# A Fourier-mixing and cosine-gated MLP kernel: another order of its opening

## The chip, the cores and the metric

The kernel runs on one core of one Trainium2 chip. The metric is the time of one execution on the device, in microseconds. A core has five engines that run side by side and wait for each other through semaphores: TensorE (PE in the profile; PEld is its loading of weights), VectorE (DVE), ScalarE (ACT), GpSimd (POOL) and SyncE (SP), which here issues nearly all DMAs. Each engine works through its own instructions in the order in which the program gives them.

## The reference

x has the shape (8, 3008, 256). Each of the 8 batches goes through a Fourier transform along its 3008 rows and another along its 256 columns, and the real part is kept. Each of the 24064 rows of 256 then goes through a small network:

```python
X = np.fft.fft(np.fft.fft(x, axis=1), axis=2).real     # (24064, 256)
h = X @ w_in                                           # w_in (256, 2048)
g = h * np.cos(h)
out = g @ w_out                                        # w_out (2048, 256)
```

All inputs and the output are float32.

## The kernel before, in words

**Transform along the rows.** 3008 is split as 47 x 64. For each batch x is loaded in four pieces (`load_x(b, p)`, L140), each with 8 of 32 forward columns and their mirrored partners; the mirrored half is read backwards in rows of 1 KB. A piece gives two chunks. `fold` (L226) adds and subtracts the two halves of the 256 columns: for batch 0 on VectorE, with GpSimd copying two columns, for later batches on GpSimd alone. `first_half` (L249) multiplies a chunk with the table `L` of length 47 into `pz` (PSUM, buffers of tag M), and `keep_z` (L285) copies it to `zs` on ScalarE. `store_z` (L322) writes zs to DRAM, and `load_z` (L334) reads it back with other axes on the partitions: z travels through DRAM. `second_half(b, g)` (L346) multiplies z with the table `BJ`, for a group g of four values of j, into `pb`; copies on ScalarE give `pq`, the transformed columns of group g. One row of pq is also spread over all partitions as `nb`, through DRAM (L376, L377) or, for the first group, by a matmul (`spread_nb`, L380).

**Transform along the columns.** It is not done on x: it is folded into w_in. `weights(e, n)` (L417) multiplies quarter n of w_in (512 of 2048 columns) with the table `CS`, giving a cosine part `WC` (e=0) and a sine part `WS` (e=1), 2 x 2 matmuls of 128 x 512 a quarter; `keep_weights` (L429) copies them to SBUF on ScalarE. Row 0 of WS holds another coefficient that is needed as columns over the partitions: `weight_row(n)` (L436) turns it with four matmuls into four columns of the tile `wn`, `keep_wn` (L449) copies these on ScalarE, and GpSimd sets the row to zero (L454).

**The main loop.** There are 8 batches x 6 groups x 8 blocks of w_in's columns = 384 steps, each in two halves; the loop (L847) runs over halves k, and t = k // 2 is the step. A half passes through a pipeline: `seed` (ScalarE, L504) writes nb times a column of wn into its PSUM tile H; `mm1` (L525) adds WC and WS products of pq; `act_e` and `dve_h` make the two mirrored values h; `act_round`, `dve_frac`, `act_sin` and `dve_g` make g = h cos h; `sums` (GpSimd, L581) makes sums of g, and `mm2` (L599) multiplies them with w_out, in combinations (`VX`, `combine_w2`, L487) that need 7 products instead of 8. mm2 of a step starts LAG = 5 halves after its first half. Half k reads column k of wn in the first group, so halves 4, 8 and 12 are the first to read what quarters 1, 2 and 3 give. The first two halves have no seed: a memset and a product with `wrow` (`seed_first`, L514) stand in for it. Halves 1 to 4 seed the next half ahead of their round (L886), later ones behind it (L894).

**The order of the work** is written out by hand, and every engine keeps it. The opening stands in lines 758 to 845: fill-in matmuls on ones (`keep_busy`), chunks, first halves, weight quarters and DMA issues; quarter 3 is folded inside the loop at k = 0, 1 and 2 (L861). `opening` (L812) is a table of calls at the end of step t. `transform(b)` (L391) is the same for the next batch: `load_x(1, p)` at t = 2p, `store_z`, `load_z` and `second_half` later. So SyncE's queue holds, one behind another: the loads of x and weights of batch 0, the stores and loads of z, quarter 3 and w_out (`load_w2`), the rest of z (j from 4 on), the rest of w_out and BJ, and then x of batch 1.

Of the kernel before, what the change touches and what calls it, by code (L numbers as in the profile page):

```python
# [11 lines left out]
FP = mybir.dt.float32  # L12
# [6 lines left out]
ND = 256  # L19
NDFF = 2048  # L20
N2 = 47
NJ = 24
# [3 lines left out]
XP = 2 * IP  # L26
NG = 6
LAG = 5
AHEAD = LAG + 1
# [79 lines left out]
def kernel(  # L109
# [7 lines left out]
    nc = tc.nc  # L117
# [22 lines left out]
    def load_x(b, p):  # L140
        if (b, p) not in xs:
            take_x(b, p)
        xt = xs[b, p]
        xv = xt.rearrange("r (i d) -> r i d", d=ND)
        i0 = XP * p
        for r0, r1 in ((0, 32), (32, 47)):
            nc.sync.dma_start(out=xv[r0:r1], in_=x_r[b, r0:r1, i0 : i0 + XP, :])
            q0, q1 = N2 + r0, N2 + r1
            if p == 0:
                nc.sync.dma_start(out=xv[q0:q1, 0:1], in_=x_r[b, r0:r1, 32:33, :])  # L150
                nc.sync.dma_start(
                    out=xv[q0:q1, 1:XP], in_=x_r[b, r0:r1, 63 : 64 - XP : -1, :]
                )
            else:
                nc.sync.dma_start(
                    out=xv[q0:q1], in_=x_r[b, r0:r1, 64 - i0 : 64 - i0 - XP : -1, :]
                )


    CS = [cpool.tile([128, 256], FP, tag=f"CS{i}", name=f"CS{i}") for i in range(2)]  # L160
    wr = [
        [spool.tile([128, 7 * 256], FP, tag=tag, bufs=1, name="wr") for tag in ("mr", "cb")],
    ]
    L = cpool.tile([128, 256], FP, tag="L", name="L")
    BJ = cpool.tile([128, NJ * 128], FP, tag="BJ", name="BJ")
    w2 = cpool.tile([128, 16 * ND], FP, tag="w2", name="w2")
# [5 lines left out]
    def load_w(q):  # L172
        for i in range(2):
            nc.sync.dma_start(
                out=wr[q // 2][i][:, 512 * (q % 2) : 512 * (q % 2) + 512],
                in_=moe_w_in[i * 128 : (i + 1) * 128, 512 * q : 512 * q + 512],
            )

    def load_bj(c0, c1):
        nc.sync.dma_start(out=BJ[:, c0:c1], in_=B_dr.ap()[:, c0:c1])  # L180
# [11 lines left out]
    load_x(0, 0)  # L192
    load_cs()
    load_w(0)
    load_x(0, 1)
    WC = cpool.tile([128, NDFF], FP, tag="WC", name="WC")
    WS = cpool.tile([128, NDFF], FP, tag="WS", name="WS")
    wn = cpool.tile([128, 16], FP, tag="wn", name="wn")
# [120 lines left out]
    zds = {}  # L319
    z2s = {}  # L320

    def store_z(b, c, j0=0, j1=NJ):  # L322
        half, q = divmod(c, NCH // 2)
        if q == 0 and j0 == 0:
            zds[b, half] = dpool.tile([32, 2 * NJ * 128], FP, tag="zd", bufs=4, name="zd")
        zd, zs = zds[b, half], zss[b, c]
        for e in range(2):
            p0 = 16 * e + IP * q
            nc.sync.dma_start(
                out=zd[p0 : p0 + IP, 256 * j0 : 256 * j1].rearrange("i (y d) -> y i d", d=128),  # L330
                in_=zs[64 * e + 2 * j0 : 64 * e + 2 * j1, :].rearrange("y (i d) -> y i d", d=128),
            )

    def load_z(b, half, j0=0, j1=NJ):  # L334
        if b not in z2s:
            z2s[b] = spool.tile([128, NJ * 128], FP, tag="z2", bufs=1, name="z2")
        for r in range(2):
            p0 = 64 * half + 32 * r
            nc.sync.dma_start(
                out=z2s[b][p0 : p0 + 32, 128 * j0 : 128 * j1].rearrange("i (j d) -> i j d", d=128),  # L340
                in_=zds[b, half].rearrange("i (j r d) -> r i j d", r=2, d=128)[r, :, j0:j1],
            )
# [71 lines left out]
    def fold_weights(e, n, tag="M"):  # L414
        keep_weights(e, n, weights(e, n, tag))

    def weights(e, n, tag="M"):  # L417
        pw = psum("pw", tag)
        for i in range(2):
            nc.tensor.matmul(  # L420
                pw,
                lhsT=CS[i][:, 128 * e : 128 * e + 128],
                rhs=wr[n // 2][i][:, 512 * (n % 2) : 512 * (n % 2) + 512],
                start=(i == 0),
                stop=(i == 1),
            )
        return pw

    def keep_weights(e, n, pw):  # L429
        W = WS if e else WC  # L430
        nc.scalar.copy(out=W[:, 512 * n : 512 * n + 512], in_=pw)

    def take_wn(n):
        keep_wn(n, weight_row(n))
# [18 lines left out]
            nc.scalar.copy(out=wrow, in_=row[:, 0:256])  # L453
        nc.gpsimd.memset(row, 0.0)  # L454

    def fold_quarter(n):
        fold_weights(1, n)
        fold_weights(0, n)
        take_wn(n)

    class Step:
        pass
# [291 lines left out]
    def chunk(c):  # L754
        fold(0, c, 0)
        fold(0, c, 1)
# [10 lines left out]
    take_wn(0)  # L767
    store_z(0, 0, 0, 4)
    store_z(0, 1, 0, 4)
    load_w(1)  # L770
    load_x(0, 2)
    load_x(0, 3)
    chunk(3)
    first_half(0, 2)
    chunk(4)
    first_half(0, 3)
    fold_quarter(1)
    store_z(0, 2, 0, 4)
    store_z(0, 3, 0, 4)
    x1 = spool.tile([128, XP * ND], FP, tag="xp", bufs=4, name="wr")  # L780
    wr.append([x1[:, 1024 * i : 1024 * i + 1024] for i in range(2)])
    load_w(2)
    load_bj(0, 512)
    store_z(0, 0, 4)
    store_z(0, 1, 4)
    chunk(5)
    first_half(0, 4)
    chunk(6)
    first_half(0, 5)
    store_z(0, 4, 0, 4)  # L790
    store_z(0, 5, 0, 4)
    chunk(7)
    first_half(0, 6)
    first_half(0, 7)
    store_z(0, 6, 0, 4)
    store_z(0, 7, 0, 4)
    for half in range(2):
        load_z(0, half, 0, 4)
    fold_quarter(2)
    keep_busy(3, "M", 256)  # L800
    load_w(3)
    load_w2(0, 2)
    load_w2(2, 4)
    for c in range(2, 8):
        store_z(0, c, 4)
    load_bj(512, 1024)
    for half in range(2):
# [3 lines left out]
    load_bj(1024, NJ * 128)  # L811
    opening = {  # L812
        0: ((combine_w2, 0, 2), (combine_w2, 2, 4)),
        3: ((combine_w2, 4, 6, 0, 2),),
        4: ((combine_w2, 4, 6, 2, 4),),
        5: ((combine_w2, 6, 8, 0, 2), (second_half, 0, 1)),
        6: ((combine_w2, 6, 8, 2, 4),),
        10: ((second_half, 0, 2), (load_ident,)),
        14: ((second_half, 0, 3),),
# [27 lines left out]
    for k in range(2 * n + LAG):  # L847
        t, u = divmod(k, 2)
        d, v = divmod(k - LAG, 2)
        cur, prev, old, nxt = unit(k), unit(k - 1), unit(k - 2), unit(k + 1)  # L850
        done = step(d)
        full = step(d if v else d - 1, True)
        if cur:
            if k % (2 * per) == 0:
                todo = transform(cur.s.b + 1) if cur.s.b + 1 < NB else {}
            if k not in range(3, AHEAD):
                mm1(cur, 0)
                if t == 0:
                    seed_first(cur)
                act_e(cur)  # L860
            if k == 0:  # L861
                spread_nb()
                fold_weights(1, 3)
            elif k == 1:
                pw = weights(0, 3)
            elif k == 2:
                pw = weight_row(3)
        pair = None if u else pairs.pop(t, None)
        if pair:
            b, c = pair  # L870
            pz = [first_half(b, c, borrow("pz"))]
        if old:
            dve_g(old)
            if old.u:
                sums(old.s)
        if pair:
            pz.append(first_half(b, c + 1, borrow("pz", 1)))
        pm = clear_middle() if u and t in middles else None
        if done:
            order = (0, 1, 5, 4, 3, 2, 6) if done is steps[-1] else range(7)  # L880
            mm2(done, 4 * v, 4 * v + 3, order)
        if pm is not None:
            middle(pm)
        if full and full is not steps[-1]:
            take_m(full, 1 if v else 3, nc.vector)
        if nxt and 0 < k < AHEAD - 1:  # L886
            seed(nxt)
        if prev:
            act_round(prev)
        if pm is not None:  # L890
            nc.scalar.copy(out=zm[64:128], in_=pm)
        if pair:
            keep_z(b, c, pz[0])
        if nxt and k >= AHEAD - 1:  # L894
            seed(nxt)
        if full and full is not steps[-1]:
            take_m(full, 0 if v else 2, nc.scalar)
        if prev:
            dve_frac(prev)
        if k + 1 in range(3, AHEAD):  # L900
            mm1(nxt, 0)
            act_e(nxt)
        copy_small()
        if prev:
            act_sin(prev)
        if pair:
            keep_z(b, c + 1, pz[1])
            patch_z(b, c)
            patch_z(b, c + 1)
        if k == 1:  # L910
            keep_weights(0, 3, pw)
        elif k == 2:
            keep_wn(3, pw)
        if cur:
            mm1(cur, 1)
        if done and v == 0:
            mm2(done, 3, 4, order)
        if cur:
            dve_h(cur)
        if u == 0:  # L920
            continue
        for i in range(6):
            s = step(t - 4 - i, True)
            if s:
                combine_m(s, i)
        for sg, lag in ((0, 8), (1, 10)):
            s = step(t - lag, True)
            if s:
                store_out(s, sg)
        for call in opening.pop(t, ()):  # L930
            call[0](*call[1:])
        for call in todo.pop(t % per, ()):
            call[0](*call[1:])
# [31 lines left out]
```

## Time and profile before

| | |
|---|---|
| three runs | 1954.88, 1955.91, 1956.15 us; median 1955.91 |
| the profiled execution | 1955.04 us, of which the span from the first to the last instruction is 1953.2 |
| busy: TensorE matmuls, weight loads | 1939.2 us (99%), 1686.3 us (86%) |
| busy: ScalarE, VectorE, GpSimd | 1509.7 (77%), 1456.8 (75%), 1396.3 us (71%) |
| DMA | 88.70 MB, 45 GB/s in the mean; 21.5% of 16 engines' span |
| mean granted TensorE clock | 0.998 |

The times are in microseconds from the start of the span. A row of a timeline gives start, duration, engine, line, operation, output <- inputs and a count; a float32 matmul shows as two. In square brackets stands how long the engine was idle before, and what ended that. SPq is SyncE's queue; a DMA's row is its issue, the transfer comes after. A row of the windows gives the stretch, the sum of its length, busy time (and count) of TensorE, weight loads, VectorE, ScalarE and GpSimd, and then the granted clock of TensorE, the busy share of the DMA engines and GB/s.

### The profile page before, as it was taken

To read this page: it belongs to the slowest core of one execution; us is meant where nothing else is said; L and a number is where in the kernel's file an instruction comes from. 1 tells how busy PE (TensorE), PEld (TensorE's weight loads), DVE (VectorE), ACT (ScalarE), POOL (GpSimd) and SP (SyncE) were. 2 spreads that over 40 slices of the span, in tenths; PEclk is the share of its full clock that TensorE was granted. 3 is DMA by queue.
4 is the path that set the end of the run, shared out by engine and by line. 5 is a ranking of instruction groups with operands and counts; after the bars stand their busy time and mean duration, and the time that the engine had idled before them with its cause. 6 is when DMAs were issued, how large, how long until landed. Compare 5 with 4: busy or idle time off the path is not lost.

```text
span 1953.2 us, 29669 instructions
## 1 busy us (share of the span) xinstructions
PE 1939.2 (99%) x9262; PEld 1686.3 (86%) x9262; DVE 1456.8 (75%) x2529; ACT 1509.7 (77%) x3450; POOL 1396.3 (71%) x1593
## 2 busy tenths in 40 slices
PE   8999999999999999999999999999999999999998
PEld 4988889888988889888898888988889888898887
DVE  3767777777777777777777777777777777788786
ACT  3777778777787787877778787788777877778775
POOL 2777767787677866787668776687767777666775
PEclk9999999999999999999999999999999999999999
DMA  8611024111230223201241112412014111100001
GB/s 195 130 30 40 22 51 79 25 36 37 52 69 18 41 41 62 49 21 40 42 82 27 37 28 41 86 24 41 21 42 86 24 38 27 39 22 16 12 16 28
DMA packets 176690, 88.70 MB, mean 45 GB/s; under 512 B 103303, under 2 KB 173622, under 8 KB 174902
## 3 DMA queue, kind: packets, MB, share of 16 engines
q1 hardware_dynamic: 176374, 86.68, 21.5%
q8 instruction: 75, 1.23, 0.3%
q14 instruction: 81, 0.66, 0.1%
q10 hardware_dynamic: 160, 0.13, 0.0%
HBM read 49.50 MB, written 37.27 MB: 44 GB/s over the span
## 4 chain that ended last, share of the span: by engine, by line
PE 98%; ACT 0%; DMA 0%; DVE 0%; SPq 0%; POOL 0%; issue 0%; POOLq 0%; ACTq 0%
PE M L620 58%; PE H L529 33%; PE pz L262 3%; PE pb L353 2%; PE pw L420 1%; DMA xp<-in_x_dram 0%; PE pz L259 0%; PE pw L440 0%; DMA wr<-in_moe_w_in_dram 0%; PE pm L310 0%; PE pd L476 0%; DVE r L561 0%; ACT r L567 0%; POOL xf L245 0%; DVE cb L687 0%; ACT r L557 0%
## 5 line engine op out<-in xcount | busy, mean ns | idle before, releaser
L587 POOL TENSOR_TENSOR S<-r 128x512 f32<-128x512 f32 (+1 forms) x383 | 474.8, 1240 | 450.4 <-DVE r L571 405.5
L561 DVE SCALAR_TENSOR_TENSOR r<-r,H 128x512 f32<-128x512 f32 (+1 forms) x768 | 518.6, 675 | 196.7 <-ACT r L557 170.4
L567 ACT ACTIVATE r<-r 128x512 f32<-128x512 f32 (+1 forms) x768 | 477.0, 621 | 242.5 <-DVE r L561 237.4
L620 PE MATMUL M<-S,VX 128*128 128x256 f32 (+1 forms) x2304 | 615.2, 376 | 0.0
L571 DVE SCALAR_TENSOR_TENSOR r<-H,r 128x512 f32<-128x512 f32 (+1 forms) x768 | 519.0, 676 | 128.9 <-ACT r L567 88.9
L620 PEld LDWEIGHTS M<-S,VX 128*128 128x128 f32 x2304 | 435.4, 190 | 71.3 <-issue 22.7
L529 PE MATMUL H<-pq,WC 128*128 128x256 f32 (+1 forms) x1536 | 453.6, 377 | 2.1 <-ACT H L510 2.1
L529 PE MATMUL H<-pq,WS 128*128 128x256 f32 (+1 forms) x1536 | 451.5, 376 | 0.0
L557 ACT ACTIVATE r<-H 128x512 f32<-128x512 f32 (+1 forms) x768 | 447.9, 583 | 0.4 <-DVE H L545 0.4
L545 DVE TENSOR_TENSOR H<-ew,H 128x256 f32<-128x256 f32 (+1 forms) x768 | 324.7, 423 | 143.0 <-PE H L529 83.5
L620 PE MATMUL M<-r,w 128*128 128x256 f32 (+1 forms) x1536 | 388.4, 375 | 0.0
L541 ACT ACTIVATE ew<-H 128x256 f32<-128x256 f32 (+1 forms) x768 | 287.2, 374 | 119.5 <-PE H L529 115.1
L510 ACT ACTIVATE H<-nb,wn 128x256 f32<-128x256 f32 (+1 forms) x766 | 366.3, 478 | 0.9
L620 PEld LDWEIGHTS M<-r,w 128*128 128x128 f32 x1536 | 300.8, 197 | 27.3
L529 PEld LDWEIGHTS H<-pq,WS 128*128 128x128 f32 x1536 | 290.3, 190 | 33.7 <-ACT ew L541 1.0
L529 PEld LDWEIGHTS H<-pq,WC 128*128 128x128 f32 x1536 | 279.2, 190 | 45.9 <-ACT H L510 11.0
L593 POOL TENSOR_TENSOR S<-S,r 128x256 f32<-128x256 f32 (+1 forms) x383 | 275.5, 719 | 30.0
L594 POOL TENSOR_TENSOR S<-r,S 128x256 f32<-128x256 f32 (+1 forms) x383 | 274.6, 717 | 30.0
L620 PE MATMUL M<-r,VX 128*128 128x256 f32 (+1 forms) x768 | 225.5, 375 | 0.0
L620 PE MATMUL M<-S,w 128*128 128x256 f32 (+1 forms) x768 | 225.2, 375 | 0.0
L620 PEld LDWEIGHTS M<-S,w 128*128 128x128 f32 x768 | 150.5, 196 | 14.6
L620 PEld LDWEIGHTS M<-r,VX 128*128 128x128 f32 x768 | 146.1, 190 | 14.7
(74 smaller groups left out, 923.4 us busy)
## 6 DMA issues: line engine op xcount, KB each, us to landing
out_dram<-ob SPq DMA_DIRECT2D x728, 32.0 KB
xp<-in_x_dram SPq DMA_DIRECT2D x56, 256.0 KB
zd<-zs SPq DMA_DIRECT2D x112, 96.0 KB
z<-zd SPq DMA_DIRECT2D x28, 384.0 KB
xp<-in_x_dram SPq DMA_DIRECT2D x56, 120.0 KB
nb<-nd SPq DMA_DIRECT2D x40, 128.0 KB
wr<-in_moe_w_in_dram SPq DMA_DIRECT2D x8, 256.0 KB
w<-in_moe_w_out_dram SPq DMA_DIRECT2D x4, 512.0 KB
```

What stands on the lines that cost most here:

```text
L510: nc.scalar.activation(out=h.H[:, 0:T], in_=s.nb[:, 0:T], func=AF.Copy, bias=0.25, scale=wn[:, f : f + 1])
L529: nc.tensor.matmul(h.H[:, 0:T], lhsT=W[:, 128 * f : 128 * f + 128], rhs=s.pq[:, e * T : e * T + T], start=False, stop=True, skip_group_che ...
L541: nc.scalar.mul(out=h.ew[:, 0:T], in_=h.H[:, 0:T], mul=2.0)
L545: nc.vector.tensor_tensor(out=h.H[:, T : 2 * T][:, ::-1], in0=h.ew[:, 0:T], in1=h.H[:, 0:T], op=ALU.subtract)
L557: nc.scalar.activation(out=r, in_=y, func=AF.Copy, bias=BIG, scale=1.0)
L561: nc.vector.scalar_tensor_tensor(out=r, in0=r, scalar=-BIG, in1=y, op0=ALU.add, op1=ALU.subtract)
L567: nc.scalar.activation(out=r, in_=r, func=AF.Sin, bias=0.0, scale=SIN_SCALE)
L571: nc.vector.scalar_tensor_tensor(out=r, in0=y, scalar=-0.25, in1=r, op0=ALU.add, op1=ALU.mult)
L587: tt(out=sv[:, 0:2], in0=qv[:, 1:2].to_broadcast([128, 2, T]), in1=qv[:, 0:4:3], op=ALU.subtract,)
L593: tt(out=sv[:, 2], in0=sv[:, 1], in1=gv[:, 0, 0], op=ALU.subtract)
L594: tt(out=sv[:, 3], in0=gv[:, 1, 0], in1=sv[:, 2], op=ALU.add)
L620: nc.tensor.matmul(acc[key][m // 2][:, 256 * (m % 2) : 256 * (m % 2) + T], lhsT=w, rhs=a, start=first, stop=s.fp == 7, skip_group_check=True,)
```

## The change

The order of the opening is written anew, and two ways of doing a thing are replaced:

- All four x pieces of batch 0 are issued before weight quarters 1 and 2 and the first columns of BJ; quarter 2 gets a place of its own in the tiles `mr` and `cb`, quarter 3 in a buffer of `r`.
- Quarters 1 and 2 are folded after all first halves, instead of between them. The filler of three matmuls before the second half goes.
- The z stores of chunks 6 and 7 are issued by ScalarE instead of SyncE. Those of chunks 0 and 1 for j from 4 on come with the others, later.
- The rows of quarters 1, 2 and 3 no longer go through `weight_row`: `send_wn` writes a row to DRAM from ScalarE's queue, and `load_wn` reads it back as columns on SyncE's, with an access of single elements. The row of quarter 3 is sent at k = 3 and loaded at t = 3.
- At k = 0 the cosine products and first seeds of halves 0 and 1 come first; the products of quarter 3 follow at k = 0 and 1, and VectorE instead of ScalarE copies them at k = 1 and 2.
- The second half of group 1 moves from t = 5 to t = 4.

```diff
--- before.py
+++ after.py
@@ -158,9 +158,12 @@
 
 
     CS = [cpool.tile([128, 256], FP, tag=f"CS{i}", name=f"CS{i}") for i in range(2)]
-    wr = [
-        [spool.tile([128, 7 * 256], FP, tag=tag, bufs=1, name="wr") for tag in ("mr", "cb")],
-    ]
+    wr = [spool.tile([128, 7 * 256], FP, tag=tag, bufs=1, name="wr") for tag in ("mr", "cb")]
+    wl = spool.tile([128, 1024], FP, tag="r", bufs=4, name="wr")
+
+    def raw(q, i):
+        return wl[:, 512 * i : 512 * i + 512] if q == 3 else wr[i][:, 512 * q : 512 * q + 512]
+
     L = cpool.tile([128, 256], FP, tag="L", name="L")
     BJ = cpool.tile([128, NJ * 128], FP, tag="BJ", name="BJ")
     w2 = cpool.tile([128, 16 * ND], FP, tag="w2", name="w2")
@@ -172,7 +175,7 @@
     def load_w(q):
         for i in range(2):
             nc.sync.dma_start(
-                out=wr[q // 2][i][:, 512 * (q % 2) : 512 * (q % 2) + 512],
+                out=raw(q, i),
                 in_=moe_w_in[i * 128 : (i + 1) * 128, 512 * q : 512 * q + 512],
             )
 
@@ -192,7 +195,11 @@
     load_x(0, 0)
     load_cs()
     load_w(0)
-    load_x(0, 1)
+    for p in (1, 2, 3):
+        load_x(0, p)
+    load_w(1)
+    load_bj(0, 512)
+    load_w(2)
     WC = cpool.tile([128, NDFF], FP, tag="WC", name="WC")
     WS = cpool.tile([128, NDFF], FP, tag="WS", name="WS")
     wn = cpool.tile([128, 16], FP, tag="wn", name="wn")
@@ -319,14 +326,14 @@
     zds = {}
     z2s = {}
 
-    def store_z(b, c, j0=0, j1=NJ):
+    def store_z(b, c, j0=0, j1=NJ, eng=nc.sync):
         half, q = divmod(c, NCH // 2)
         if q == 0 and j0 == 0:
             zds[b, half] = dpool.tile([32, 2 * NJ * 128], FP, tag="zd", bufs=4, name="zd")
         zd, zs = zds[b, half], zss[b, c]
         for e in range(2):
             p0 = 16 * e + IP * q
-            nc.sync.dma_start(
+            eng.dma_start(
                 out=zd[p0 : p0 + IP, 256 * j0 : 256 * j1].rearrange("i (y d) -> y i d", d=128),
                 in_=zs[64 * e + 2 * j0 : 64 * e + 2 * j1, :].rearrange("y (i d) -> y i d", d=128),
             )
@@ -420,15 +427,15 @@
             nc.tensor.matmul(
                 pw,
                 lhsT=CS[i][:, 128 * e : 128 * e + 128],
-                rhs=wr[n // 2][i][:, 512 * (n % 2) : 512 * (n % 2) + 512],
+                rhs=raw(n, i),
                 start=(i == 0),
                 stop=(i == 1),
             )
         return pw
 
-    def keep_weights(e, n, pw):
+    def keep_weights(e, n, pw, copy=nc.scalar.copy):
         W = WS if e else WC
-        nc.scalar.copy(out=W[:, 512 * n : 512 * n + 512], in_=pw)
+        copy(out=W[:, 512 * n : 512 * n + 512], in_=pw)
 
     def take_wn(n):
         keep_wn(n, weight_row(n))
@@ -453,10 +460,18 @@
             nc.scalar.copy(out=wrow, in_=row[:, 0:256])
         nc.gpsimd.memset(row, 0.0)
 
-    def fold_quarter(n):
-        fold_weights(1, n)
-        fold_weights(0, n)
-        take_wn(n)
+    wds = {}
+
+    def send_wn(n):
+        row = WS[0:1, 512 * n : 512 * n + 512]
+        wds[n] = dpool.tile([1, 512], FP, tag="wd", bufs=3, name="wd")
+        nc.scalar.dma_start(out=wds[n], in_=row)
+        nc.gpsimd.memset(row, 0.0)
+
+    def load_wn(n):
+        nc.sync.dma_start(
+            out=wn[:, 4 * n : 4 * n + 4], in_=wds[n].rearrange("o (k p) -> (o p) k", p=128)
+        )
 
     class Step:
         pass
@@ -767,41 +782,35 @@
     take_wn(0)
     store_z(0, 0, 0, 4)
     store_z(0, 1, 0, 4)
-    load_w(1)
-    load_x(0, 2)
-    load_x(0, 3)
     chunk(3)
     first_half(0, 2)
     chunk(4)
     first_half(0, 3)
-    fold_quarter(1)
     store_z(0, 2, 0, 4)
     store_z(0, 3, 0, 4)
-    x1 = spool.tile([128, XP * ND], FP, tag="xp", bufs=4, name="wr")
-    wr.append([x1[:, 1024 * i : 1024 * i + 1024] for i in range(2)])
-    load_w(2)
-    load_bj(0, 512)
-    store_z(0, 0, 4)
-    store_z(0, 1, 4)
     chunk(5)
     first_half(0, 4)
     chunk(6)
     first_half(0, 5)
     store_z(0, 4, 0, 4)
     store_z(0, 5, 0, 4)
+    load_z(0, 0, 0, 4)
     chunk(7)
     first_half(0, 6)
+    store_z(0, 6, 0, 4, nc.scalar)
     first_half(0, 7)
-    store_z(0, 6, 0, 4)
-    store_z(0, 7, 0, 4)
-    for half in range(2):
-        load_z(0, half, 0, 4)
-    fold_quarter(2)
-    keep_busy(3, "M", 256)
+    store_z(0, 7, 0, 4, nc.scalar)
+    load_z(0, 1, 0, 4)
+    for n in (1, 2):
+        fold_weights(1, n)
+        send_wn(n)
+        fold_weights(0, n)
+    load_w2(0, 2)
     load_w(3)
-    load_w2(0, 2)
     load_w2(2, 4)
-    for c in range(2, 8):
+    load_wn(1)
+    load_wn(2)
+    for c in range(8):
         store_z(0, c, 4)
     load_bj(512, 1024)
     for half in range(2):
@@ -811,9 +820,9 @@
     load_bj(1024, NJ * 128)
     opening = {
         0: ((combine_w2, 0, 2), (combine_w2, 2, 4)),
-        3: ((combine_w2, 4, 6, 0, 2),),
-        4: ((combine_w2, 4, 6, 2, 4),),
-        5: ((combine_w2, 6, 8, 0, 2), (second_half, 0, 1)),
+        3: ((combine_w2, 4, 6, 0, 2), (load_wn, 3)),
+        4: ((combine_w2, 4, 6, 2, 4), (second_half, 0, 1)),
+        5: ((combine_w2, 6, 8, 0, 2),),
         6: ((combine_w2, 6, 8, 2, 4),),
         10: ((second_half, 0, 2), (load_ident,)),
         14: ((second_half, 0, 3),),
@@ -853,18 +862,19 @@
         if cur:
             if k % (2 * per) == 0:
                 todo = transform(cur.s.b + 1) if cur.s.b + 1 < NB else {}
-            if k not in range(3, AHEAD):
+            if k >= AHEAD:
                 mm1(cur, 0)
-                if t == 0:
-                    seed_first(cur)
                 act_e(cur)
             if k == 0:
+                for h in (cur, nxt):
+                    mm1(h, 0)
+                    seed_first(h)
+                    act_e(h)
                 spread_nb()
-                fold_weights(1, 3)
-            elif k == 1:
-                pw = weights(0, 3)
-            elif k == 2:
-                pw = weight_row(3)
+            if k < AHEAD - 1:
+                mm1(cur, 1)
+            if k == 0:
+                pw = [weights(1, 3)]
         pair = None if u else pairs.pop(t, None)
         if pair:
             b, c = pair
@@ -897,9 +907,11 @@
             take_m(full, 0 if v else 2, nc.scalar)
         if prev:
             dve_frac(prev)
-        if k + 1 in range(3, AHEAD):
+        if k + 1 in range(2, AHEAD):
             mm1(nxt, 0)
             act_e(nxt)
+        if k == 1:
+            pw.append(weights(0, 3))
         copy_small()
         if prev:
             act_sin(prev)
@@ -907,16 +919,16 @@
             keep_z(b, c + 1, pz[1])
             patch_z(b, c)
             patch_z(b, c + 1)
-        if k == 1:
-            keep_weights(0, 3, pw)
-        elif k == 2:
-            keep_wn(3, pw)
-        if cur:
+        if cur and k >= AHEAD - 1:
             mm1(cur, 1)
         if done and v == 0:
             mm2(done, 3, 4, order)
         if cur:
             dve_h(cur)
+        if k in (1, 2):
+            keep_weights(2 - k, 3, pw[k - 1], nc.vector.tensor_copy)
+        elif k == 3:
+            send_wn(3)
         if u == 0:
             continue
         for i in range(6):
```

## The prediction

> **What bounds the kernel now.** I read the page first: its chain of work that ended last is TensorE for 98%, so a microsecond of TensorE idle or extra TensorE work anywhere is a microsecond of the run, and after the opening nothing is changed. Then I read the timelines of the first 75 us, engine by engine.
>
> ```profile
> PE 98%; ACT 0%; DMA 0%; DVE 0%; SPq 0%; POOL 0%; issue 0%; POOLq 0%; ACTq 0%
> ```
>
> VectorE's timeline gives the arrival of x (pieces 1, 2, 3 of batch 0, one group of four folds each), TensorE's what it does with it:
>
> ```profile
> 14.13 2.48 DVE L234 TENSOR_TENSOR xf<-xp 94x508 f32<-94x508 f32 x4 [3.80 <-DMA xp<-in_x_dram]
> 21.95 2.51 DVE L234 TENSOR_TENSOR xf<-xp 94x508 f32<-94x508 f32 x4 [5.35 <-DMA zd<-zs]
> 26.03 2.48 DVE L234 TENSOR_TENSOR xf<-xp 94x508 f32<-94x508 f32 x4 [1.57 <-DMA xp<-in_x_dram]
> ```
> ```profile
> 29.63 3.70 PE L420 MATMUL pw<-wr,CS 128*128 128x512 f32 x8
> 33.26 1.05 PE L440 MATMUL pw<-ones,WS 1*128 1x1 f32 x8
> 34.24 1.56 PE L476 MATMUL pd<-VX 128*128 128x256 f32 x6
> 35.74 1.13 PE L353 MATMUL pb<-BJ,z 128*128 128x128 f32 x8
> ...
> 45.14 1.05 PE L440 MATMUL pw<-ones,WS 1*128 1x1 f32 x8
> ...
> 68.23 0.55 PE L529 MATMUL H<-pq,WC 128*128 128x225 f32 x2
> ```
>
> The last x piece, 26.03, sets the first halves, then a weight quarter (3.63 us), its row (1.0) and filler (1.5) run before the second half `pb` at 35.74. The row at 68.23 is the first product of half 12 (loop index 12), which I use as the finish line: from there the work is the same in both kernels, and TensorE is busy for 10.00 of every 10 us. Half 12 is seeded by ScalarE, and SyncE's queue around it reads:
>
> ```profile
> 66.37 0.45 ACT L510 ACTIVATE H<-nb,wn 128x225 f32<-128x225 f32 x1
> ```
> ```profile
> 50.13 1.20 SPq L180 DMA_DIRECT2D BJ<-dft_B  x1
> ...
> 57.43 0.32 SPq L147 DMA_DIRECT2D xp<-in_x_dram  x1
> 62.11 0.33 SPq L155 DMA_DIRECT2D xp<-in_x_dram  x1
> 63.58 0.33 SPq L147 DMA_DIRECT2D xp<-in_x_dram  x1
> 63.95 0.41 SPq L155 DMA_DIRECT2D xp<-in_x_dram  x1
> 65.00 0.93 SPq L147 DMA_DIRECT2D xp<-in_x_dram  x1
> ```
> ```profile
> SPq L155 <- DMA BJ<-dft_B: 4.3, 1, 4.3
> ```
>
> SyncE stands at 62.11 for the 1 MB of BJ, issued eight places before. The semaphore records say why: DMAs take eight semaphores in turn, and an issue waits until the DMA eight places before it has landed. Below, "landed" is the last update of a DMA's semaphore. From 34 to 73 us the transfers never run dry; this queue is the second bound of the opening.
>
> **The change, part by part.**
>
> *x ahead of the weights.* Pieces follow each other by 26.03 - 21.95 = 4.08 us. From 14.13 they now arrive at 18.2 and 22.2 instead of 26.03. Folds and first halves take 29.63 - 26.03 = 3.6 us after that: last first half done at 25.8. Weights behind x: CS and quarter 0 (768 KB) took 2.5 us from landing to landing (7.72 to 10.20), so quarter 1, BJ and quarter 2 (1280 KB) take 4.1 and are there at 23.8 to 26.3, in time.
>
> *Two quarters folded while z travels.* 2 x 3.63 = 7.3 us: 25.8 + 7.3 = 33.1 for `pb`. Two weight rows (2 x 1.0) and the filler (1.5) leave this path. z's travel is beside it: last copy 26.5; four issues by ScalarE of 0.3 each (SyncE's of this size), landing 1.5 after issue (the stores at 31.38 and 31.68), while SyncE's twelve earlier stores stand behind quarter 2 (26.3) and take 0.4 each; so the last two loads go out at 29.8 to 30.7 and land 1.9 after that (those at 32.03 to 33.61): 31.7 to 32.7. If that cover goes, `pb` follows z. So `pb` starts at 33.1, not 35.74: -2.6.
>
> *Loop head.* The row product at 45.14 (1.05) goes, its copy with it; the cosine products and seeds of halves 0 and 1 come first and the products of quarter 3 move one unit later, with their copies (0.6 each) on VectorE, which has room (busy 4.64 of 10 us from 40 to 50). By the durations of before, the third sine, 49.37 before, comes at about 46.0: -3.3, of which 0.7 is from here (bounds 0 and 1.1).
>
> *Rows through DRAM.* A row goes out on ScalarE's queue and comes back on SyncE's as 4 columns. GpSimd's clearing of the row (L454) now waits for the write to land; behind it stand the sums, with 2 to 3 us to spare. Row 1 is wanted by the seed of half 4, about 44; its load stands behind 1.5 MB of W2 and quarter 3, landing 7.6 us after the first of them was issued (34.08 to 41.70): 30.7 + 7.6 + 1 = 39. Row 2 is wanted at 54. Both hidden.
>
> *Row 3 is not.* Its load is issued at the end of t=3, so behind batch 1's x pieces 0 and 1, and the seed of half 12 reads it. Before, this place in SyncE's queue is between 63.95 and 65.00; the x DMAs ahead of it landed at 69.55, so it would land about 69.8. The shift of this queue: SyncE reaches the first big load right after the last z load, at about 30.7 instead of 34.08, -3.4. Against that, four z stores that ran at 25.9 to 27.5 now stand after it: 4 x 0.38 (landing spacing of such stores) = +1.5. Each row load moves 512 single elements, 32 on each of 16 engines; no such row exists. By the packet records, 4-byte semaphore writes (9 ns) give 0.3 from below, 1 KB packets (88 ns) 2.8 from above. I take the smallest data packets, 256 B at 18 ns, nearest in size: 0.6, and 1.8 for three loads. Row 3 lands at 69.8 - 3.4 + 1.5 + 1.8 = 69.7. The Trainium skill speaks against this load (DMA: Bandwidth & Descriptors, Rules for kernel authors): a strided last dimension becomes one descriptor per element. It gives no price per element, and no run here shows one.
>
> The seed wants it at 66.37 - 3.3 + 1.0 = 64.1; the 1.0 is the second half of group 1, now ahead of it (t=4) instead of behind (67.34). So ScalarE stands 5.6 us at a wait that replaces the one removed; queued behind it are all sines and seeds, and TensorE runs out within half a microsecond. The product of half 12 starts at 69.7 + 0.5 = 70.2 against 68.23: **+2.0**. And a clock loss:
>
> ```profile
> 50.00:60.00 10.00, 9.66 (x42) 9.24 (x43) 6.96 (x13) 6.80 (x17) 5.13 (x7) 0.83 1.13 292
> ```
>
> Granted clock (third number from the right) 0.83 over 10 us is one stretch of 3.4 us at half speed, after TensorE's thin work at 44 to 50; it costs at most 1.7. The new gap of over 5 us should bring a second: 0 to 1.7, I take 0.9.
>
> **Sum:** +2.0 + 0.9 = +2.9 against the profiled execution's 1955.04 (span 1953.2 and 1.84 around it): 1957.9. The median shown is 1955.91, 0.87 above it; on that footing, which the rivals' times have too, 1958.8. This kernel's measurement can tell about 0.2%, 3.9 us, from no change: 1952.0 to 1959.8 is "same".
>
> **Rivals.**
>
> *A, row 3 comes in time.* The 1 KB row at 69.05 landed in 2.0 us amid the same backlog. That one ran on one engine; row 3 needs all 16, hence I doubt it. If it passes the x pieces, it lands 2.0 after issue, at about 65.7, or earlier if the backlog shrinks more. Then -3.3 and a wait of at most 1.6 remain: 1952.6 to 1954.2; with the head so dense that the half-speed stretch goes too (-1.7), 1950.9. Chance 0.22, over half of it beyond 0.2%.
>
> *B, ScalarE's queue stands at its own issue (slower).* Eight semaphores serve both queues. In the tail ScalarE's two DMAs hold places two and four of the turn although the program writes them sixth and eighth, so the turn goes nearly by time, and eight places back from the write of row 3 (46) is a z store landed by 44. If it went by program order, eight back is the last-but-one W2 load, 57.36 before, and 57.36 - 3.4 + 1.5 + 1.2 = 56.7 now. ScalarE would resume at 57.0 what it did at 49.85 before: +7.2, row 3 then hidden: 1963.1. It decides as soon as that place's DMA lands after 46. The Trainium skill (same page, Anatomy of one DMA) puts the semaphore wait on the issuing sequencer, before dispatch; the trace has nothing queued behind such an issue on ScalarE. Chance 0.12.
>
> *C, single elements are dear.* If single elements cost what 1 KB packets do, 2.8 us a load, row 3 comes 3 x 2.2 = 6.6 later: +2.9 + 6.6 = +9.5, 1965.4; half-way 1962.1. For it speaks that columns 128 elements apart leave nothing to merge, against it that packets under 512 B were the cheapest. The rule of the Trainium skill quoted above is the same mechanism. Chance 0.14.
>
> **Chances and range.** The forecast case has 0.52: with row 3 landing from 66 (-1.7) to 71.5 (+3.8, and up to 1.7 of clock) it runs from 1954.2 to 1961.4, 0.41 of it same and 0.11 slower. With A (0.13 faster, 0.09 same), B (0.12 slower), C (0.12 slower, 0.02 same): faster 0.13, same 0.52, slower 0.35. The range leaves out the ends of A and of C, 1952 to 1964.
>
> **What would show it.** Right: folds of the last x piece at 22.2; `pb` at 33.1; the third sine at 46; no weight-row matmul but the first; ScalarE idle several us before the seed of half 12, ended by a DMA into wn; a second half-clock stretch. Wrong: `pb` after 33.6 with TensorE waiting for z (z's travel was priced too low); ScalarE idle just before its own write of a row (B); no wait for wn (A).

## The result, and the profile after

The changed kernel takes 1962.23 us (median of 9 runs, 1959.54 to 1962.97) against 1955.91 before (9 runs): a ratio of 1.0028, 95% interval 1.0019 to 1.0037. It is slower, since the interval lies above 1. Whether by more than the 0.2% that the prediction called "same" stays open: the middle of the interval is above it, its lower end just below. The medians alone differ by 6.3 us, 0.32%. The profiled execution took 1961.15 us with a span of 1959.4 (before 1955.04 and 1953.2).

The page still puts nearly all of the chain that ended last on TensorE, but one per cent less than before, and DMAs, which had 0%, now have 2%:

```profile
PE 97%; DMA 2%; SPq 0%; ACT 0%; DVE 0%; issue 0%; POOL 0%; POOLq 0%; ACTq 0%
```

VectorE's timeline (arrival of x, pieces 1 to 3), and TensorE's from the weight quarters to the second half and at half 12:

```profile
15.18 2.48 DVE L241 TENSOR_TENSOR xf<-xp 94x508 f32<-94x508 f32 x4 [4.39 <-DMA xp<-in_x_dram]
20.02 2.48 DVE L241 TENSOR_TENSOR xf<-xp 94x508 f32<-94x508 f32 x4 [2.37 <-DMA xp<-in_x_dram]
24.55 2.48 DVE L241 TENSOR_TENSOR xf<-xp 94x508 f32<-94x508 f32 x4 [2.05 <-DMA xp<-in_x_dram]
```
```profile
28.15 7.13 PE L427 MATMUL pw<-wr,CS 128*128 128x512 f32 x16
35.31 1.13 PE L360 MATMUL pb<-BJ,z 128*128 128x128 f32 x8
...
73.11 1.12 PE L544 MATMUL H<-pq,WC 128*128 128x225 f32 x2 [7.69 <-ACT H L525]
```

The last piece is folded at 24.55 instead of 26.03, and `pb` starts at 35.31 instead of 35.74. Then half 12 comes at 73.11 instead of 68.23, behind 7.69 us in which TensorE has nothing to do. ScalarE's timeline and the waits of SyncE's queue say why:

```profile
72.61 0.45 ACT L525 ACTIVATE H<-nb,wn 128x225 f32<-128x225 f32 x1 [8.18 <-DMA wn<-wd]
```
```profile
SPq L155 <- DMA BJ<-dft_B: 3.5, 1, 3.5
SPq L177 <- DMA wd<-WS: 3.1, 1, 3.1
```
```profile
34.04 4.00 SPq L177 DMA_DIRECT2D wr<-in_moe_w_in_dram  x2
...
38.90 1.05 SPq L472 DMA_DIRECT2D wn<-wd  x2
...
68.19 0.39 SPq L472 DMA_DIRECT2D wn<-wd  x1
```

The seed of half 12 was ready to go at 72.61 - 8.18 = 64.43 (it ran at 66.37 before) and waited 8.18 us for row 3, whose load went out at 68.19. By the semaphore records that load landed at 72.59, 0.19 us behind batch 1's x piece 1 (72.40). And SyncE stood 3.1 us at the second load of quarter 3, which nobody had foreseen: that load takes the semaphore of ScalarE's write of row 2, issued at 34.22 and landed only at 37.68.

The windows show what followed the gap (third number from the right: granted clock):

```profile
66.00:72.00 6.00, 0.00 (x0) 0.00 (x0) 0.00 (x0) 0.00 (x0) 3.35 (x5) 0.88 0.82 161
72.00:78.00 6.00, 4.89 (x15) 4.46 (x16) 1.98 (x4) 2.87 (x7) 0.00 (x0) 0.55 0.76 118
```

The clock was at half speed from 70.56 to 77.39, of which 4.28 us under work. From half 12's first product to that of half 16 it took 83.68 - 73.11 = 10.57 us, before 76.69 - 68.23 = 8.46: 2.1 lost. So, in these two executions, half 12 is 4.9 later, half 16 7.0 later; in the remaining 1880 us 0.8 came back in a few steps of 0.1 to 0.35, and 6.1 is the difference of the spans. Those 0.8 are no scatter: from half 40 to the end every profile with the changed opening takes 1814.0 to 1814.3 us, both with the old one 1815.0 to 1815.1. So from half 12 on the work is not quite the same, as the prediction took it to be; why was not looked into.

### The profile page after: what moved, and what is told of

It reads as the page before. It is cut to its first block, busy times and chain, and to the rows that moved or that the text cites. A ratio compares the mean times of both kernels' runs of the same rounds, so it can differ in the third digit from the quotient of the medians.

```text
span 1959.4 us, 29620 instructions
## 1 busy us (share of the span) xinstructions
PE 1935.2 (99%) x9232; PEld 1682.9 (86%) x9232; DVE 1457.9 (74%) x2531; ACT 1509.4 (77%) x3445; POOL 1396.9 (71%) x1593
## 4 chain that ended last, share of the span: by engine, by line
PE 97%; DMA 2%; SPq 0%; ACT 0%; DVE 0%; issue 0%; POOL 0%; POOLq 0%; ACTq 0%
PE M L635 58%; PE H L544 33%; PE pz L269 3%; PE pb L360 2%; DMA xp<-in_x_dram 2%; PE pw L427 1%; DMA z<-zd 0%; DMA wn<-wd 0%; PE pz L266 0%; PE pm L317 0%; DVE cb L702 0%; SPq L147 0%; PE H L531 0%; ACT ob L740 0%; PE pd L491 0%
```

## The experiments

The theory: what is lost is the wait of half 12's seed for row 3, whose load stands in SyncE's queue behind batch 1's x, and a half-speed clock after the gap. Rivals: the price of the single elements, SyncE's new stand, and the clock having another cause. Ratios are to the kernel before, measured beside each on the same chip; its medians there were 1955.1 to 1955.4. Nothing of the computation is left out in any of them.

**Row 3 ahead of batch 1's x** (`row3_early`), in the changed kernel:

```diff
-            at(2 * p, load_x, b, p)
+            at(1 if b == 1 and p == 0 else 2 * p, load_x, b, p)
...
-    load_bj(1024, NJ * 128)
     opening = {
+        1: ((load_wn, 3), (load_bj, 1024, NJ * 128)),
...
-        3: ((combine_w2, 4, 6, 0, 2), (load_wn, 3)),
+        3: ((combine_w2, 4, 6, 0, 2),),
```

> The changed kernel, but row 3 is loaded at the end of t=1, ahead of the last megabyte of BJ and of batch 1's x (both issued after it). Theory (the loss is the seed of half 12, which waits 8.2 us for a row that stands behind these transfers, and the half-speed clock after that wait): no wait of ScalarE for wn, no half-speed stretch in the opening; the third sine stays at about 48.0, 1.4 ahead of before, and the half-speed stretch that before has at 50.6 (worth up to 1.7) stays away too: 1955.9 - 1.4 - 1.7 = 1952.8, at worst 1954.5. Rival (x first and z's way make the opening late as a whole, the wait only shows it): ScalarE then waits elsewhere, for nb or x, and the time stays above 1959.

1955.76 us, ratio 1.0000 (0.9991 to 1.0009). In the profile the wait of half 12 is gone (seed at 62.71, no idle time before it), and so is the half-speed stretch. In its place stands a new wait, four halves on, in ScalarE's timeline:

```profile
69.10 0.46 ACT L525 ACTIVATE H<-nb,wn 128x225 f32<-128x225 f32 x1
74.71 0.48 ACT L525 ACTIVATE H<-nb,wn 128x256 f32<-128x256 f32 x1 [3.55 <-DMA nb<-nd]
```

The row `nb` of group 1 travels through DRAM behind the same x pieces. The loss was the wait for row 3, and what was behind it in line is the next wait. But this profile, at 1952.82 us and so where I had expected the median, is of one of the two fastest among eleven executions. Those two have a mean granted clock of 0.999, the other nine 0.997 to 0.998 at 1954.2 to 1956.9 us. One stretch of 3.41 us is 0.001 of that mean, so most executions had one or two; where they lay, no trace shows.

**The second half of group 1 ahead of x too** (`row3_nb_early`): the kernel above, with

```diff
-            at(1 if b == 1 and p == 0 else 2 * p, load_x, b, p)
+            at((1, 4, 5, 6)[p] if b == 1 else 2 * p, load_x, b, p)
```

> The kernel with row 3's load moved up (row3_early), and with the x pieces of batch 1 loaded later, so that the second half of group 1 travels ahead of them too. Nothing is left out. Theory (the order of the queue alone makes the loss: what the seeds of halves 12 and 16 read stands behind x that nobody wants yet): the 3.55 us wait before the seed of half 16 goes, no wait takes its place, and the time is 1952 to 1953, about 3 us under the kernel before, since the opening's 2 to 3 us of gain are kept. Rival (the gain of the opening is paid back anyhow, by the next transfer that is late: now batch 1's x): the time stays at 1955.8 and a wait for xp or a fold behind it shows after 75 us.

1950.23 us, ratio 0.9974 (0.9962 to 0.9985): faster than both kernels. ScalarE's timeline has no wait at either seed (half 12, half 16):

```profile
62.84 0.45 ACT L525 ACTIVATE H<-nb,wn 128x225 f32<-128x225 f32 x1
...
71.25 0.48 ACT L525 ACTIVATE H<-nb,wn 128x256 f32<-128x256 f32 x1
```

The rows travel through DRAM as in the changed kernel; only their place in the queue is another. Against the kernel before, half 40 is 138.15 - 133.62 = 4.5 us earlier: 2.9 by the third sine (46.52 against 49.37), and 1.7 because no half-speed stretch fell into this opening (before: 50.61 to 54.02).

**The rows turned by TensorE again**, all three (`rows_by_tensor`: `take_wn` in the opening, `weight_row(3)` at k = 2, `keep_wn` at k = 3, no `send_wn` and `load_wn`):

> The changed kernel with all rows 1 to 3 turned by TensorE as before the change, nothing through DRAM. Theory: the wait at half 12 is gone; three row products cost 3 x 1.0 on TensorE, and SyncE's stand of 3.1 us for the write of row 2 (34.5 to 37.7) is gone as well: 1952.8 + 3.0 = 1955.8, between 1954 and 1957. Rival (order of the loads is what costs): 1959 or more.

1952.1 us, ratio 0.9982 (0.9973 to 0.9991): below the 1954 to 1957 that I had expected. No seed waits and half 12 starts at 66.39. So the rest of the change, without the rows' way through DRAM, is a gain of 0.18%; with that way as it was put, a loss of 0.28%. In the profile little of that gain is a shorter opening: the third sine comes at 49.07, 0.3 ahead of before; the other 1.5 at half 12 fall where before has its half-speed stretch, and here there is none.

**Row 3 alone by TensorE** (`row3_by_tensor`: rows 1 and 2 through DRAM and sent ahead of both cosine products, x pieces of batch 1 at t = 0, 4, 5, 6):

> The changed kernel with row 3 alone turned into columns by TensorE again (eight products of one column at k=2), the writes of rows 1 and 2 ahead of the cosine products, and batch 1's x pieces loaded later as in the kernel above. Nothing is left out. Theory: no seed waits for a DMA; half 12 starts at 63.5 to 65 instead of 68.2 and the half-speed stretch is gone or short; 1950 to 1952. Rival (turning rows on TensorE costs what it saves): 1.05 us for the product and its copy delays, as in the kernel with all rows on TensorE, 1952 to 1953.

1950.59 us, ratio 0.9973 (0.9962 to 0.9983). Half 12 starts at 65.04. It has a half-speed stretch of 3.41 us, from 47.63, which I had expected short or gone. It is level with the kernel that keeps all rows in DRAM and reorders the queue.

**Row 3 through DRAM alone**, in the kernel before (`row3_alone`: `send_wn(3)` at k = 2 and `load_wn(3)` at t = 3 in place of `weight_row` and `keep_wn`):

> The kernel before, with one part of the change: row 3 goes through DRAM, written by ScalarE at k=2 and loaded by SyncE at t=3; everything else stays. Theory: row 3 lands right behind batch 1's x piece 1, at about 69.8 (x landed at 69.55 in before), ScalarE waits some 4 us at the seed of half 12; its product starts at 70.3 instead of 68.23, +2.1, and a second half-speed stretch adds 1 to 1.7: 1959 to 1960. Rival (the new order of the opening is to blame): no wait, one row product less, 1955.

1957.91 us, ratio 1.0017 (1.0008 to 1.0026), below the 1959 to 1960 expected. The seed of half 12 waited 1.08 us for the row, but in the profile this wait costs TensorE nothing: half 12 follows the second half of group 1 without a gap. What costs there is the row's write. ScalarE issued it at 48.56, and by the semaphore records it landed at 55.37, 6.8 us later. GpSimd's clearing of the row waited for that landing (released at 55.40), the sums `S` stand behind the clearing, and TensorE ran out for 1.19 us:

```profile
48.56 0.46 ACTq L461 DMA_DIRECT2D wd<-WS  x1
55.48 0.52 POOL L462 MEMSET WS<- 1x512 f32 x1 [8.62 <-ACT r L580]
57.07 0.65 PE L633 MATMUL M<-S,VX 128*128 128x225 f32 x2 [1.19 <-POOL S L600]
...
70.12 1.05 PE L353 MATMUL pb<-BJ,z 128*128 128x128 f32 x8
71.01 0.55 PE L542 MATMUL H<-pq,WC 128*128 128x225 f32 x2
```

(The release named in the second row is the sine that ended at about the same time.) Half 40 is 2.8 later than before: 1.4 of that is there at `pb` already (37.14), up to which the code is the same, and so is scatter of this execution; 1.2 is the gap. So this run shows that row 3's way through DRAM costs time in the kernel before too, but not that the seed's wait is what costs. The 2 to 3 us that the prediction had to spare behind the clearing were not enough here; in the changed kernel the write landed after 2.0 us (48.01 to 49.99), and they were.

**x piece 1 later** (`x1_later`), one edit in the changed kernel:

```diff
-            at(2 * p, load_x, b, p)
+            at((0, 4, 5, 6)[p] if b == 1 else 2 * p, load_x, b, p)
```

> The changed kernel with one edit: batch 1's x piece 1 (four DMAs, 752 KB) is loaded at t=4 and not at t=2, so that row 3 stands behind piece 0 alone. Nothing is left out. Theory (row 3 lands when what is ahead of it in the queue has landed; the DMAs ahead of it landed at 69.52 for piece 0 and 72.40 for piece 1 in the trace of the changed kernel): row 3 lands about 2.9 us earlier, the wait before the seed of half 12 falls from 8.2 to about 5.3 us, and the time falls by 2.5 to 3 us, to a ratio of about 1.0013 to the kernel before. Rival (the wait is for the row's own write and its small packets, however long the queue): no change.

1957.01 us, ratio 1.001 (1.0002 to 1.0019), with this wait:

```profile
69.02 0.45 ACT L525 ACTIVATE H<-nb,wn 128x225 f32<-128x225 f32 x1 [5.77 <-DMA wn<-wd]
```

Row 3 landed 36.6 us after the first load of W2 was issued, in the changed kernel 39.0: 2.5 earlier for 752 KB less ahead of it. The two kernels below that only add work for TensorE have the same queue and show how much this time scatters: 40.2 with six products, 39.9 with nine. The wait follows the length of the queue.

**The gap filled, six products** (`gap_filled`):

```diff
             send_wn(3)
+        if k == 11:
+            pd = borrow("pd")
+            for i in range(6):
+                nc.tensor.matmul(
+                    pd, lhsT=WC[:, 0:128], rhs=WC[:, 0:512], start=i == 0, stop=i == 5
+                )
```

> The changed kernel plus six 128x512 products without use, queued on TensorE behind half 11, so that its gap of 7.7 us at 65.4 holds 5.4 us of work. Theory (6.8 us at half speed after the gap cost about 2 us on top of the wait): the seed still waits for row 3, the half-speed stretch is gone or at least halved, 1960 to 1961. Rival (the clock falls for another reason, or the stretch hides behind other waits): 1962.2 as without.

1960.78 us, ratio 1.0027 (1.0017 to 1.0036). A gap of 3.84 us was left, and the clock was at half speed for 6.83 us all the same: nothing decided. It did show the opening at its best: `pb` at 33.27 and the third sine at 45.86, 2 us earlier than in the profile of the changed kernel, and yet half 12 at 72.26, only 0.9 earlier. The queue's big loads began 2.0 earlier as well (31.56), but row 3 landed 40.2 us after that instead of 39.0. Where the seed waits for the queue, an earlier opening is worth what it does for the queue.

**The gap filled, nine products** (`gap_filled_9`, the same with `range(9)`):

> The changed kernel with nine filler products of 128x512 behind half 11 (six left a gap of 3.84 us and the clock still fell). They should cover the whole gap, 9 x 0.9 = 8.2 us. Theory (the half-speed stretch behind the wait is the gap's, and costs some 2 us on top of the wait): no stretch at half speed after 70 us, half 12 starts as before, and half 16 follows it by 8.5 us instead of 10.6; the time is 2 us under the changed kernel, 1960.2. Rival (the stretch is not the gap's): the clock falls all the same and the time is that of the changed kernel, 1962.2, or above it where the filler runs past the landing of row 3.

1958.87 us, ratio 1.0018 (1.001 to 1.0027). TensorE's timeline, where only 0.80 of the gap is left, and the windows:

```profile
64.67 7.89 PE L935 MATMUL pd<-WC 128*128 128x512 f32 x18
73.36 0.65 PE L544 MATMUL H<-pq,WC 128*128 128x225 f32 x2 [0.80 <-ACT H L525]
```
```profile
72.00:78.00 6.00, 5.20 (x26) 4.58 (x25) 3.29 (x6) 4.21 (x10) 1.06 (x1) 1.00 0.86 137
```

Half 12 starts as late as in the changed kernel (73.36), the seed waits as long (9.0 us), the clock stays at 1.00, and half 16 follows 8.48 us later instead of 10.57. The ratios differ by 0.10%, 2.0 us. Their intervals overlap, but size and traces agree: the clock's part is 2.1 us and it is the gap's.

**Row 2 sent earlier** (`sines_first`):

```diff
     for n in (1, 2):
         fold_weights(1, n)
         send_wn(n)
+    for n in (1, 2):
         fold_weights(0, n)
```

> The changed kernel, but with the sine products of quarters 1 and 2 and the writes of their rows ahead of both cosine products, so that row 2 is sent some 2 us earlier (its write went out at 34.2 and landed at 37.7, and SyncE stood 3.1 us at the second load of quarter 3 for it). Theory (the end of the opening is set by when SyncE's queue brings row 3, and that stand is one of its terms): the stand falls from 3.1 to about 1 us, everything behind it comes up to 2 us earlier, row 3 with it, and the time falls by 1 to 2 us against the changed kernel, to 1960 to 1961.3. Rival (the DMA engines have work in hand during the stand and the backlog is what counts): the stand goes and the landing of row 3 and the time stay, 1962.

1959.36 us, ratio 1.0022 (1.0013 to 1.0031). SyncE's waits:

```profile
SPq L346 <- DMA wd<-WS: 2.8, 1, 2.8
```

The stand at L177 is gone, and another of 2.8 us has come: the last z load takes the semaphore of ScalarE's write of row 3, which landed 4.1 us after its issue. Row 3 landed 38.7 us after the first load of W2 was issued, 39.0 in the changed kernel: 0.3 us less, and less than the scatter of this time (39.0 to 40.2 with the queue unchanged). So no gain in the queue is shown. That is what the rival said, but as one stand took the place of the other, the run does not tell what a queue without a stand would gain; the 0.06% between the ratios are within their intervals.

**The price of single elements** (`rows_five_times`: `load_wn(1)` and `load_wn(2)` five times each):

> The changed kernel with the loads of rows 1 and 2 issued five times each, to the same columns: eight more loads of 512 single elements. Nothing is left out. Theory (a load of 512 single elements takes 0.19 us of the queue, the spacing of the two landings in the trace of the changed kernel): row 3 lands 8 x 0.19 = 1.5 us later, the time rises by as much. My estimate on record (0.6 each) gives 4.8 us, and the rival of dear single elements (2.8 each) 22 us. SyncE's own issue of a row load took 0.5 us, so if the queue is short of issues there, the eight cost up to 4 us for that reason, with SyncE's times showing it.

1971.97 us, ratio 1.0083 (1.007 to 1.0097). This does not measure what it should: each load waited for the landing of the one before into the same columns, some 2.1 us each (SyncE: 6.7 us of waits for wn). It shows that such a load alone takes 2.1 us from issue to landing.

**The same to columns of their own** (`spare_loads`):

```diff
     load_wn(2)
+    wx = cpool.tile([128, 32], FP, tag="wx", name="wx")
+    for i in range(8):
+        nc.sync.dma_start(
+            out=wx[:, 4 * i : 4 * i + 4],
+            in_=wds[1 + i % 2].rearrange("o (k p) -> (o p) k", p=128),
+        )
```

> The changed kernel with eight more loads of 512 single elements behind those of rows 1 and 2, each to columns of its own that nobody reads, so that none waits for another's landing (with the same columns as target, each waited some 2 us for the one before, and row 3 came 8.8 us later for that alone). Nothing is left out. Theory (0.19 us of the queue each): row 3 lands 1.5 us later against the first load of W2 than in the changed kernel (39.0 us after that load was issued there, 40.5 here), and the time is 1 to 2 us above the changed kernel, a ratio of 1.0033 to 1.0040 to the kernel before. My estimate on record (0.6 each) gives 4.8 us and a ratio near 1.005; dear elements (2.8 each) 22 us and 1.014.

1967.98 us, ratio 1.0063 (1.0049 to 1.0076). Row 3 landed 44.6 us after the first load of W2 was issued, 5.6 more than in the profile of the changed kernel and 4.4 more than the latest with the same queue (40.2): 0.55 to 0.70 a load. My theory of 0.19 is wrong for these; the prediction's 0.6 is near, and 2.8 is far off. SyncE's timeline, and the windows (last two numbers: share of the DMA engines, GB/s), say what the price is:

```profile
39.75 5.06 SPq L815 DMA_DIRECT2D wx<-wd  x8
```
```profile
42.00:44.00 2.00, 2.00 (x8) 1.21 (x7) 1.48 (x3) 1.35 (x4) 1.37 (x3) 1.00 0.57 4
44.00:46.00 2.00, 1.55 (x7) 0.87 (x5) 1.67 (x5) 1.15 (x4) 1.47 (x3) 1.00 0.53 6
```

SyncE needs 0.51 us to issue one. Right behind the big load of W2 they landed 0.17 to 0.20 apart; when the queue had run out, 0.50 to 0.60 apart, with the DMA engines little over half busy. It is the issue that costs where the queue is short; the elements cost the 0.17 to 0.20. The packet records say so too: against the changed kernel the eight loads add 4224 packets of 4 bytes, 8 x 512 and 128 semaphore writes, so each element is a packet of its own, and such a packet takes 9 ns (median). The time rose by 6.8 us (0.0063 - 0.0028 = 0.35%), since this execution has a new TensorE gap of 3.36 us that ends at 64.4 (the second half of group 1 waits for its z, which stands behind the eight loads) and two more half-speed stretches besides.

**All early** (`all_early`: `row3_nb_early` with the loop of `sines_first`):

> The kernel with row 3 and the second half of group 1 ahead of batch 1's x, and also with both sine products and row writes of quarters 1 and 2 ahead of the cosine products. Nothing is left out. Theory (no transfer is late any more, TensorE's order alone counts): SyncE's stand for row 2 goes and the time stays at that of row3_nb_early, a ratio of 0.997 to the kernel before. Rival (the second halves of group 0 were late by what SyncE stood): up to 1 us less, 0.9965.

1950.33 us, ratio 0.9978 (0.9969 to 0.9987): no more gained. SyncE's stand for a row's write did not go but moved, from 3.2 us at the second load of quarter 3 to 2.5 us at the last z load, so what such a stand costs where no seed waits for the queue is not shown. That it does not make the loss, `row3_nb_early` shows: it has the stand of 3.2 us and is faster than the kernel before.

## Why the prediction was right or wrong

The mechanism was right: the one wait that replaced the one removed is ScalarE's for row 3, behind batch 1's x, with a half-speed stretch after the gap. Its size was not: +2.9 forecast, +6.1 in the profiled spans, +6.3 in the medians. The median lies within the range, but 0.8 us beyond the end that I gave to the likeliest case alone. That the range holds it is luck: what it has above 1961.4 was there for the rivals B and C, and neither happened. By the median the outcome is "slower" (0.35) and not "same" (0.52); the interval of the ratio, 1.0019 to 1.0037, just reaches into "same".

- *x ahead of the weights:* forecast 22.2 for the last piece, measured 24.55. **This is the first term that failed.** I took the 4.08 us of one execution as the spacing of the pieces; here it was 4.84 and 4.53. And I took piece 1 over from before at 14.13; it came at 15.18, which is 1.1 of the 2.3 us. In eight profiled executions of kernels with this very opening the last fold starts at 22.6 to 24.6, in the mean 23.5. The old opening scatters as well: 26.03 in the profile before, 27.53 in that of `row3_alone`.
- *From there to `pb`:* the last first half ends 3.7 us after the fold (3.6 forecast), and the quarters take 7.1 (7.3). `pb` at 35.31 and not 33.1 is the x pieces' lateness. The cover held, barely: the last z load landed at 35.11 (semaphore records), 0.2 us ahead of `pb`; 0.4 to 1.4 were forecast.
- *Loop head:* from `pb` to the third sine 12.7 us, before 13.6: -0.9, forecast -0.7. So the third sine came at 48.0, not at 46.0.
- *Start of the big loads in SyncE's queue:* forecast 30.7, measured 33.56. This is the same lateness and 0.5 more for z's travel (0.4 in the kernel with six filler products: 31.56 after a last fold at 22.63).
- *From there to the landing of row 3:* 35.7 + 1.5 + 1.8 = 39.0 forecast, 39.0 measured. That it is exact is luck: the same queue took 39.9 and 40.2 in two other executions. Nor was every part right. The elements are packets of 9 ns and not of 18, so that a row load costs 0.2 us behind other transfers, and 0.5 to 0.7 where SyncE's issue sets the pace; for three loads that is 0.6 to 1.6 instead of 1.8, depending on how many of them meet a short queue. And SyncE's stand for row 2's write, which I had not seen, is in the 39.0 with a part that no run tells. I had looked for the turn of eight semaphores on ScalarE only (rival B); it bit on SyncE.
- *The wait:* wanted at 64.43 (forecast 64.1), landed at 72.59 (69.7): 8.2 instead of 5.6, half 12 +4.9 instead of +2.0. That the wanted time is so near is luck: the third sine was 2.0 late, and from there to the seed it took 16.4 us instead of the 18.0 that the sum had, since the half-speed stretch that before has at 50.61, and that I had kept in the sum, did not come.
- *The clock:* +0.9 forecast with 1.7 as the most, 2.1 measured. **This is the second term that failed:** I took one stretch of 3.4 us as the longest; after a gap of this length it was two, 6.83. The nine filler products show that these two hang on the gap.

Of the rivals, A (row 3 passes the x pieces) did not happen: it landed 0.19 us behind the last of them. B did not happen: ScalarE had no idle time before its write of row 3 at 48.01. C is refuted by the spare loads: at most 0.70 us against 2.8, and by the packets of 9 ns. The Trainium skill says that a strided last dimension lowers to one descriptor per element (DMA: Bandwidth & Descriptors, Rules for kernel authors). The trace agrees, with one packet of 4 bytes for each element; in loads as small as these they cost less (0.17 to 0.20 us) than the issue (0.51).

So where did the gain go? The opening earned 1.9 us at the seed of half 12 (64.43 against 66.37), and up to 4.1 in other executions (62.29 in the kernel with six filler products). All of it, and more, was given back at one seed, since what that seed reads had been put into a queue behind batch 1's x pieces 0 and 1, 752 KB each, which nothing read before 82 us. With the queue in another order the gain stays: 0.26%.

## What to carry to other kernels

When a small operand is moved from an engine to a DMA, the price is its place in the queue: list what stands ahead of it and when each landed, and put it ahead of everything that is wanted later. When one wait is taken away, look for the next reader of the same queue (here `nb`, four halves on) before counting the gain. Look at the write as well: what waits for it to land (here the clearing on GpSimd, and the sums behind that) can be late before the reader is. A time that hangs on DMA arrival should be taken from several executions, not from one.

## What the runs showed of the hardware that I had not expected

- **The clock.** Half-speed stretches came in multiples of 3.41 us (3.41, 6.83, and 10.24 once, in `rows_five_times`), and their length does not follow the gap's: a TensorE gap of 3.05 us gave none, 3.84 gave 6.83, 5.29 gave 3.41, 7.69 gave 6.83. The Trainium skill (TensorE: Matmul & The Clock Gate, What's actually happening) has it that activity is judged in free-running windows of 3413 ns. These traces agree: 5.29 us that end just as the stretch begins (69.53 and 69.60) cost one window, 7.69 that end 2.6 us into it (73.11 and 70.56) cost two.
- **The semaphores in turn.** A write of 2 KB from ScalarE's queue landed after 1.1 us when the queue was short and after 3.1 to 4.1 when big loads were under way (6.8 in `row3_alone`); and since both queues share the eight semaphores, SyncE stood 2.5 to 3.2 us for it (3.8 in `row3_alone`), though it needed nothing of that write.
- **Scatter of DMA.** The same opening put its last x piece at 22.6 to 24.6 us, while the 1814 us from half 40 to the end repeat within 0.3 us in all kernels with the changed opening. What makes it so was not looked into.
